# Leftover keys and values in half rows, AV over two PSUM banks, and batch 1's attention one block later, in a kernel of pooled attention and an MLP

## The chip, the cores and the metric

One core of one Trainium2 chip. The metric is the device time of the whole launch in microseconds (us), less is better. The kernel before takes 300.76 us (median of 3 runs, 300.65 to 300.78). All runs quoted here are of the fast state (some executions are slower at a lower granted clock, whatever the kernel; none of those is used); the profile's span is some 1.7 us shorter than the time.

## The reference

Eight batches of eight heads with 576 rows of 64. Keys and values are averaged over groups of 8 rows, so each head has 72 pooled keys. The attention output, 4608 tokens of 512, goes through an MLP with `h - tanh(h)` between its two products.

```python
k_p = k.reshape(B, H, Sp, pool, D).mean(axis=3)      # Sp = 72, pool = 8
v_p = v.reshape(B, H, Sp, pool, D).mean(axis=3)
attn = softmax(scale * q @ k_p.T)                    # (cut) max subtracted, 1e-9 added to the sum
x = (attn @ v_p).transpose(0, 2, 1, 3).reshape(B * S, H * D)
h = x @ w_in                                         # 512 -> 2048
return (h - np.tanh(h)) @ w_out                      # 2048 -> 512
```

## The kernel before

AV is the product of the attention weights and the pooled values; to "turn" a block is to transpose it on TensorE. PSUM, where TensorE writes, has eight banks. The MLP works on nine groups of 512 tokens. One group is a hidden phase (16 blocks of four matmuls of 512 columns) and an output phase (16 output blocks of four). The attention of batch 0 comes first, with nothing to hide it: this is the prelude. Batch 1's attention is hidden in group 0's output phase, the later ones in later groups. Two heads of pooled keys are 144 rows; 128 fill the partitions and 16 are "left". A batch has 4 pairs of heads, so 64 left rows. The queries of a head are 512 rows and a "tail" of 64.

```python
def load_dense(src, dst, b, eng=nc.sync):            # left rows of batch 0: 64 partitions, 2 KB each
    return eng.dma_start(out=dst[0 : NM * LO, NM, :], in_=src[b, 128:PR, :, :])

def load_q_tail(b, t, eng):                          # 64 rows x 8 heads: 512 pieces of 256 B
    eng.dma_start(out=t[:QT, :, R, :], in_=q[b, :, QA:S, :].rearrange("h p d -> p h d"))

def av_half(b, blk, half, x_sb, alloc):              # (cut) three matmuls into one PSUM bank, then
    nc.vector.reciprocal(out=rden[:, :, :], in_=ps[:, :, D:D1])
    nc.vector.tensor_tensor(out=x_sb[:, half, :, :], in0=ps[:, :, 0:D],
                            in1=rden[:, :, :].to_broadcast([128, 4, D]), op=ALU.mult)
# ... prelude (cut): ScalarE's program order
scores_wide(0, (0, 1))
nc.scalar.dma_start(out=t0[:QT, :, R, :], ...)       # batch 0's query tail, on ScalarE's queue
q_turn(nc.scalar.copy, 4, 6)
# ...
load_w2(0)                                           # GpSimd's queue: w1 in 4 chunks, then w2
load_w2(1)
after(load_k(1), w1_dmas[1])                         # SyncE: batch 1's keys once w1's 2nd chunk is in
load_q(1, False)
load_main(v_pairs, v_raw[1], 1, 0, NM)
# ... hidden phase of group 0
nc.scalar.copy(out=q_bf[:QT, R, :, :], in_=t0[:QT, :, R, :])   # cast of the tail, before block 0
for i in range(5, NHID):
    mlp_h(0, i, gts)
    if i == 7:  q_pe_tail(0)                         # its transposes
    if i == 9:  scores_tail(0)
    if i == 11: x4 = av(0, 4, ps_any, False)
    if i == 13: x_pe_transpose(0, 4, x4)
for u in range(16):                                  # output phase of group 0, batch 1 inside
    mlp_o(0, u % 4, (u // 4) * 4, (u // 4) * 4 + 4, gts, o_pools[u % 4])
    if u == 2: k_transpose(1, ...)
    # (cut)
    if u >= 11: x_pe_transpose(1, *pend.pop(0))
    # (cut)
```

Of the kernel before, what the change touches and what calls it, by code (L numbers as in the profile page):

```python
# [15 lines left out]
POOL = 8  # L16
# [3 lines left out]
R = 4  # L20
QA = 128 * R
QT = S - QA
T = B * S
# [14 lines left out]
def kernel(  # L38
# [19 lines left out]
    ps_h = ctx.enter_context(tc.tile_pool(name="ps_h", bufs=3, space=PSUM))  # L58
    ps_o = ctx.enter_context(tc.tile_pool(name="ps_o", bufs=2, space=PSUM))
    ps_a = ctx.enter_context(tc.tile_pool(name="ps_a", bufs=3, space=PSUM))  # L60
# [9 lines left out]

    w1b = const.tile([128, NFB, DFF], BF16, name="w1b")
# [3 lines left out]
    spread = const.tile([128, 128], BF16, name="spread")  # L75
    mask = const.tile([128, 3 * NM, 1], FP32, name="mask")
# [3 lines left out]
    q_bf = const.tile([128, R + 1, H, D], BF16, name="q_bf")  # L80
    warm = const.tile([128, 1], FP32, name="warm")
# [22 lines left out]
    def load_left(src, dst, b, eng=nc.sync):  # L104
        return [
            eng.dma_start(out=dst[32 * t : 32 * t + LO, NM, :], in_=src[b, 128:PR, t, :])
            for t in range(NM)
        ]
# [5 lines left out]

    def load_k(b):
        return [
            load_main(k_pairs, k_raw[b % 2], b, 0, NM),
            load_dense(k_pairs, k_raw[b % 2], b),
        ]

    def load_v(b):
        return [load_main(v_pairs, v_raw[b % 2], b, 0, NM)] + load_left(
            v_pairs, v_raw[b % 2], b
        )

    def load_q_tail(b, t, eng):
        eng.dma_start(
            out=t[:QT, :, R, :], in_=q[b, :, QA:S, :].rearrange("h p d -> p h d")
        )

    def load_q(b, tail=True):
        if b not in q_raws:
            q_raws[b] = raw.tile([128, H, R + 1, D], FP32, name="q_raw", tag="q_raw")
        t = q_raws[b]
        nc.sync.dma_start(
            out=t[:, :, 0:R, :], in_=q[b, :, 0:QA, :].rearrange("h (p j) d -> p h j d", j=R)
        )
        if tail:
            load_q_tail(b, t, nc.sync)
# [4 lines left out]
    def q_cast(b, eng=nc.gpsimd.tensor_copy, parts=1):  # L144
        t = q_raws.pop(b)
        n = H // parts
        for h in range(0, H, n):
            eng(  # L148
                out=q_bf[:, 0:R, h : h + n, :].rearrange("p j h d -> p h j d"),
                in_=t[:, h : h + n, 0:R, :],  # L150
            )
        eng(out=q_bf[:QT, R, :, :], in_=t[:QT, :, R, :])

    def q_dma_transpose(b):
        qT = work.tile([128, NHP, S], BF16, name="qT", tag="qT")
        for j in range(R + 1):
            rows = 128 if j < R else QT
            nc.sync.dma_start_transpose(
                out=qT[:, :, j * 128 : j * 128 + rows],
                in_=q_bf[:rows, j, :, :].rearrange("p h d -> p (h d)"),  # L160
            )
        qTs[b] = qT

    def q_pe_transpose(b, hps, eng=None):
        if b not in qTs:
            qTs[b] = work.tile([128, NHP, S], BF16, name="qT", tag="qT")
        qT = qTs[b]
        for hp in hps:
            ps = ps_any([128, QA], FP32, "qT_ps")
            for j in range(R):  # L170
                nc.tensor.matmul(  # L171
                    ps[:, j * 128 : (j + 1) * 128],
                    lhsT=q_bf[:, j, 2 * hp : 2 * hp + 2, :].rearrange("p h d -> p (h d)"),
                    rhs=ident[:, :],
                    start=True,
                    stop=True,
                )
            evac(qT[:, hp, 0:QA], ps[:, :], eng)

    def q_pe_tail(b):  # L180
        ps = ps_any([128, NHP, QT], FP32, "qt_ps")
        for hp in range(NHP):
            nc.tensor.matmul(
                ps[:, hp, :],
                lhsT=q_bf[:, R, 2 * hp : 2 * hp + 2, :].rearrange("p h d -> p (h d)"),
                rhs=ident[:, 0:QT],
                start=True,
                stop=True,
            )
        evac(qTs[b][:, :, QA:S], ps[:, :, :])  # L190

# [22 lines left out]
    def pool_v(b, eng):  # L214
# [10 lines left out]
        v_main(VB[b % 2], r[:, :, 0:1, :], eng, 0, NM)  # L225
        v_left(VB[b % 2], r[:, NM, 0:1, :], eng)

    def v_main(vb, vs, eng, t0, t1):
# [3 lines left out]
            in0=vs[:, t0:t1, :, :].to_broadcast([128, n, 2, D]),  # L232
# [4 lines left out]
        )  # L237

# [27 lines left out]

    def k_transpose(b, alloc, engs=(nc.vector.tensor_copy, nc.scalar.copy)):
# [5 lines left out]
        ps = alloc([128, 128], FP32, "kT_ps")  # L273
        turn_tile(ps[:, :], kd, NM)
# [18 lines left out]
    def score_mms(b, t, dst, c0, c1, pairs=range(NM)):  # L293
        for m in pairs if t == NM else (t,):
# [11 lines left out]
    def scores(b, t):  # L306
        if t == 0:
            E_tiles[b] = work.tile([128, NT, S], BF16, name="E", tag="E")
        E = E_tiles[b]
        hs = S // 2  # L310
        pss = []
        for half in range(2):
            ps = ps_a.tile([128, hs], FP32, name="s_ps", tag="ps_a")
            score_mms(b, t, ps[:, :], half * hs, (half + 1) * hs)
            pss.append(ps)
        for half, ps in enumerate(pss):
            nc.scalar.activation(  # L317
                out=E[:, t, half * hs : (half + 1) * hs], in_=ps[:, :], func=ACT.Exp, scale=SCALE
            )

    def scores_wide(b, ts):
# [3 lines left out]
        for t in ts:  # L325
            ps = ps_any([128, QA], FP32, "s_ps")
            score_mms(b, t, ps[:, :], 0, QA)
# [10 lines left out]
    def av_half(b, blk, half, x_sb, alloc):  # L338
        E = E_tiles[b]
        vb = VB[b % 2]  # L340
        c0 = blk * 128 if blk < 4 else S - 128
        ps = alloc([128, 4, D1], FP32, "x_ps")
        for n in range(3):
# [14 lines left out]
        rden = work.tile([128, 4, 1], FP32, name="rden", tag="rden", bufs=4)  # L358
        nc.vector.reciprocal(out=rden[:, :, :], in_=ps[:, :, D:D1])  # L359
        nc.vector.tensor_tensor(  # L360
            out=x_sb[:, half, :, :],
            in0=ps[:, :, 0:D],
            in1=rden[:, :, :].to_broadcast([128, 4, D]),
            op=ALU.mult,
        )
# [33 lines left out]
    def out_segments(c0, nrows):  # L399
        segs = []  # L400
        r = 0
        while r < nrows:
            c = c0 + r
            bb = c // S
            i = c % S
            if i < QA:
                j = i // 128
                p0 = i % 128
                ln = min(128 - p0, nrows - r, QA - i)
                dst = out[bb * S : bb * S + QA, :].rearrange("(p j) m -> p j m", j=R)[  # L410
                    p0 : p0 + ln, j, :
                ]
            else:
                ln = min(S - i, nrows - r)
                dst = out[bb * S + i : bb * S + i + ln, :]
# [6 lines left out]
    def mlp_h_mms(g, i, f0, f1, pool=None):  # L422
        tok0 = g * TG
        if f0 == 0:
            p, tag = pool or (ps_h, "hT_ps")
            h_tiles[i] = p.tile([128, TG], FP32, name="hT_ps", tag=tag)
# [96 lines left out]
    warm_ps = ps_o.tile([128, 512], FP32, name="warm_ps", tag="o_ps")  # L523
# [7 lines left out]
    t0 = raw.tile([128, H, R + 1, D], FP32, name="q_raw", tag="q_raw")  # L531

    def load_q0(h0, h1):
        return nc.scalar.dma_start(
            out=t0[:, h0:h1, 0:R, :],
            in_=q[0, h0:h1, 0:QA, :].rearrange("h (p j) d -> p h j d", j=R),
        )

    nc.vector.memset(zeros, 0.0)  # L539
    nc.vector.memset(k_raw[0][:, NM, :], 0.0)  # L540
    nc.vector.memset(v_raw[1][:, NM, :], 0.0)
    load_main(k_pairs, k_raw[0], 0, 0, 1)
    load_q0(0, 2)
    load_main(k_pairs, k_raw[0], 0, 1, 2)
    load_q0(2, 4)
    load_main(k_pairs, k_raw[0], 0, 2, 4)
    load_q0(4, 8)
    load_dense(k_pairs, k_raw[0], 0, nc.scalar)
    load_dense(v_pairs, v_raw[1], 0, nc.scalar)
# [7 lines left out]
    nc.gpsimd.memset(q_bf[64:128, R, :, :], 0.0)  # L557
# [16 lines left out]
    for i in range(2):  # L574
        nc.gpsimd.tensor_scalar_mul(VB[i][:, :, D:D1], mask[:, :, :], float(POOL))
    nc.gpsimd.dma_start(out=v_bf[:, 0:NM, :], in_=v_pairs[0, 0:128, :, :])  # L576
    nc.gpsimd.memset(spread[:, :], 0.0)
    nc.gpsimd.tensor_copy(
        out=spread.rearrange("p (t x) -> p t x", x=32)[:, :, 0:LO],
        in_=ident[:, 0 : NM * LO].rearrange("p (x t) -> p t x", t=NM),  # L580
# [4 lines left out]
    nc.gpsimd.tensor_copy(out=v_bf[:, NM, :], in_=v_raw[1][:, NM, :])  # L585
    load_w2(1)
    nc.gpsimd.memset(k_raw[1][:, NM, :], 0.0)
    nc.gpsimd.memset(v_raw[0][:, NM, :], 0.0)
    nc.gpsimd.memset(KB[1][:, :], 0.0)

    q_raws[1] = raw.tile([128, H, R + 1, D], FP32, name="q_raw", tag="q_raw")
    after(load_k(1), w1_dmas[1])
    load_q(1, False)
    load_main(v_pairs, v_raw[1], 1, 0, NM)

# [6 lines left out]
    def k_turn_left():  # L602
        ps = ps_any([128, 128], FP32, "kT_ps")
        turn_tile(ps[:, :], kdups[0], NM)
# [4 lines left out]
    def q_turn(eng, h0, h1):  # L609
        eng(  # L610
            out=q_bf[:, 0:R, h0:h1, :].rearrange("p j h d -> p h j d"),
            in_=t0[:, h0:h1, 0:R, :],
        )

    def v_pe_pool(t0, t1, turn):
        ps = ps_any([128, t1 - t0, 1, D], FP32, "v_ps")
        for j in range(POOL):
# [187 lines left out]
```

## Time and profile before

| kernel before | us |
|---|---|
| time, median of 3 runs | 300.76 |
| batch 0's first AV matmul | 14.61 |
| first hidden matmul of group 1, by the chain | 55.02 |
| the same, by its start in TensorE's timeline | 54.98 |
| span of the profile | 299.1 |

The prediction below shows the lines that carry the bound. Three lines that it did not look at matter afterwards. First two of ScalarE's timeline, then one of TensorE's (start, length, engine, line, operation, out<-in, shapes; in brackets the idle time before it and what ended it; ACTq and SPq are issues of transfers):

```profile
8.12 0.65 ACTq L640 DMA_DIRECT2D q_raw<-in_q_dram  x1
21.03 0.62 ACT L691 CAST q_bf<-q_raw 64x512 bf16<-64x512 f32 x1
```

```profile
26.02 0.28 PE L183 MATMUL qt_ps<-ident,q_bf 128*128 128x64 bf16 x4
```

There is no bracket on the last two. Batch 0's query tail, issued at 8.12 us on ScalarE's queue, lands 8.1 us later, and is long there when ScalarE casts it at 21.03 and when TensorE turns it at 26.02.

### The profile page before, as it was taken

What the parts mean: (1) busy time and instruction counts of PE and PEld (TensorE: products, weight loads), DVE (VectorE), ACT (ScalarE), POOL (GpSimd) and SP (SyncE); (2) the same over time, 40 slices, a digit from 0 to 9 for tenths busy, and PEclk for the clock granted to TensorE, in tenths of its full rate; (3) what the DMA queues carried; (4) which work ended last, traced back from release to release, by engine and by line L of the source; (5) the groups of instructions that cost most, each with busy time, mean ns of one, the idle gap of its engine ahead of it and who ended that gap; (6) DMA issues with size and microseconds to landing.
All of it is one profiled execution on the core that took longest, in us unless ns stands there. A gap on an engine that the chain in (4) does not pass through costs nothing.

```text
span 299.1 us, 4694 instructions
## 1 busy us (share of the span) xinstructions
PE 291.5 (97%) x1671; PEld 142.5 (48%) x1671; DVE 159.1 (53%) x343; ACT 149.4 (50%) x283; POOL 115.5 (39%) x110
## 2 busy tenths in 40 slices
PE   7989999999999999999999999999999999999994
PEld 3454455544544454445444554455445544444443
DVE  5658665673547444753476247716680758108600
ACT  4647583666146633654265516650665166126511
POOL 8500904871496109922971089307940000000000
PEclk9999999999999999999999999999999999999999
DMA  7999999849854998699648974897431430111032
GB/s 251 226 211 278 311 227 310 263 87 328 234 113 99 271 297 134 117 302 245 107 88 235 300 167 94 242 294 159 97 66 35 95 92 0 37 70 36 0 72 70
DMA packets 66183, 49.79 MB, mean 166 GB/s; under 512 B 39920, under 2 KB 52976, under 8 KB 66160
## 3 DMA queue, kind: packets, MB, share of 16 engines
q1 hardware_dynamic: 58832, 42.94, 56.0%
q0 software_dynamic: 4752, 4.72, 9.4%
q10 hardware_dynamic: 2576, 1.84, 2.3%
q8 instruction: 13, 0.21, 0.3%
q14 instruction: 10, 0.08, 0.1%
HBM read 36.70 MB, written 9.44 MB: 154 GB/s over the span
## 4 chain that ended last, share of the span: by engine, by line
PE 85%; DMA 9%; POOL 4%; issue 0%; SPq 0%; ACT 0%; DVE 0%; POOLq 0%
PE o_ps L456 40%; PE hT_ps L428 37%; DMA w1b<-in_moe_w_in_dram 4%; PE x_ps L346 4%; DMA k_raw<-in_k_dram 4%; PE s_ps L298 3%; POOL k_raw L198 1%; DMA out_dram<-o_sb 1%; POOL k_raw L203 1%; POOL kd L206 1%; POOL w2b L510 0%; PE xT_ps L390 0%; POOL v_raw L576 0%; PE qT_ps L171 0%; POOL w1b L503 0%
## 5 line engine op out<-in xcount | busy, mean ns | idle before, releaser
L456 PE MATMUL o_ps<-w2b,gT 128*128 128x512 bf16 x560 | 134.4, 380 | 0.0
L441 DVE TENSOR_TENSOR gT<-hT_ps,t_sb 128x512 bf16<-128x512 f32 x144 | 98.9, 691 | 57.7 <-ACT t_sb L439 57.6
L428 PE MATMUL hT_ps<-xT,w1b 128*128 128x512 bf16 x576 | 126.9, 379 | 0.3 <-ACT xT L397 0.3
L439 ACT ACTIVATE t_sb<-hT_ps 128x512 f32<-128x512 f32 x144 | 85.6, 597 | 38.3 <-PE hT_ps L428 37.5
L428 PEld LDWEIGHTS <-w1b 128*128 128x128 bf16 x576 | 55.9, 98 | 66.5 <-issue 0.4
L456 PEld LDWEIGHTS <-gT 128*128 128x128 bf16 x560 | 52.5, 98 | 52.0 <-issue 1.4
L465 ACT COPY o_sb<-o_ps 128x512 f32<-128x512 f32 x33 | 19.3, 585 | 75.2 <-PE o_ps L456 75.2
L359 DVE RECIPROCAL rden<-x_ps 128x4 f32<-128x4 f32 x80 | 14.2, 177 | 52.5 <-PE x_ps L346 52.0
L360 DVE TENSOR_TENSOR x_sb<-x_ps,rden 128x256 bf16<-128x256 f32 x80 | 34.0, 425 | 3.5 <-DMA xT<-x_sb 0.6
L148 POOL CAST q_bf<-q_raw 128x2048 bf16<-128x2048 f32 x6 | 11.3, 1888 | 59.9 <-issue 34.8
L198 POOL TENSOR_TENSOR k_raw<-k_raw 128x1280 f32<-128x1280 f32 x7 | 20.2, 2886 | 27.4 <-DMA k_raw<-in_k_dram 16.6
L317 ACT ACTIVATE E<-s_ps 128x288 bf16<-128x288 f32 x60 | 21.4, 410 | 13.2 <-PE s_ps L298 13.0
L346 PE MATMUL x_ps<-VB,E 128*128 128x130 bf16 x240 | 20.8, 221 | 0.4 <-ACT xT L397 0.3
L346 PEld LDWEIGHTS <-E 128*128 128x128 bf16 x240 | 16.9, 98 | 8.8 <-DVE VB L230 0.6
L216 POOL TENSOR_TENSOR v_raw<-v_raw 128x1280 f32<-128x1280 f32 x6 | 17.4, 2898 | 0.0
L298 PE MATMUL s_ps<-qT,KB 128*128 128x288 bf16 (+5 forms) x128 | 17.0, 290 | 0.2
L298 PEld LDWEIGHTS <-KB 128*128 128x128 bf16 (+1 forms) x128 | 7.0, 96 | 10.2 <-issue 3.5
L527 PE MATMUL warm_ps<-xT 128*128 128x512 bf16 x29 | 10.2, 465 | 1.3 <-DVE xT L539 1.3
L206 POOL TENSOR_TENSOR kd<-k_raw 128x640 bf16<-128x640 f32 x7 | 10.8, 1540 | 0.5
L203 POOL TENSOR_TENSOR k_raw<-k_raw 128x640 f32<-128x640 f32 x7 | 10.8, 1541 | 0.5
L397 ACT CAST xT<-xT_ps 128x256 bf16<-128x256 f32 (+1 forms) x14 | 5.8, 436 | 8.5 <-PE xT_ps L390 5.1
L219 POOL TENSOR_TENSOR v_raw<-v_raw 128x640 f32<-128x640 f32 x6 | 9.3, 1544 | 0.5
(73 smaller groups left out, 100.7 us busy)
## 6 DMA issues: line engine op xcount, KB each, us to landing
k_raw<-in_k_dram SPq DMA_DIRECT2D x7, 1024.0 KB, 5.9
q_raw<-in_q_dram SPq DMA_DIRECT2D x7, 1024.0 KB, 10.2
v_raw<-in_v_dram SPq DMA_DIRECT2D x7, 1024.0 KB, 9.3
out_dram<-o_sb SPq DMA_DIRECT2D x38, 128.0 KB, 2.4
out_dram<-o_sb SPq DMA_DIRECT2D x16, 256.0 KB, 3.7
w1b<-in_moe_w_in_dram POOLq DMA_DIRECT2D x4, 512.0 KB, 14.2
w2b<-in_moe_w_out_dram POOLq DMA_DIRECT2D x4, 512.0 KB, 16.9
k_raw<-in_k_dram SPq DMA_DIRECT2D x7, 128.0 KB, 5.8
```

The source lines that it names most:

```text
L198: first = eng.tensor_tensor(out=r[:, :, 0:4, :], in0=r[:, :, 0:4, :], in1=r[:, :, 4:8, :], op=ALU.add)
L216: eng.tensor_tensor(out=r[:, :, 0:4, :], in0=r[:, :, 0:4, :], in1=r[:, :, 4:8, :], op=ALU.add)
L298: nc.tensor.matmul(dst[p : p + w], lhsT=KB[b % 2][:, o : o + w], rhs=qTs[b][:, m, c0:c1], start=True, stop=True,)
L317: nc.scalar.activation(out=E[:, t, half * hs : (half + 1) * hs], in_=ps[:, :], func=ACT.Exp, scale=SCALE)
L346: nc.tensor.matmul(ps[:, 2 * n : 2 * n + 2, :].rearrange("p h d -> p (h d)") if n < 2 else ps.rearrange("p (a s) d -> p a s d", s=2)[:, :, ...
L359: nc.vector.reciprocal(out=rden[:, :, :], in_=ps[:, :, D:D1])
L360: nc.vector.tensor_tensor(out=x_sb[:, half, :, :], in0=ps[:, :, 0:D], in1=rden[:, :, :].to_broadcast([128, 4, D]), op=ALU.mult,)
L428: nc.tensor.matmul(h_tiles[i][:, :], lhsT=w1b[:, fb, i * 128 : (i + 1) * 128], rhs=xT[:, fb, tok0 : tok0 + TG], start=(fb == 0), stop=(fb ...
L439: nc.scalar.activation(out=t_sb[:, :], in_=h_ps[:, :], func=ACT.Tanh)
L441: nc.vector.tensor_sub(out=gT[:, :], in0=h_ps[:, :], in1=t_sb[:, :])
L456: nc.tensor.matmul(o_ps[:, :], lhsT=gts[i][:, tb * 128 : (tb + 1) * 128], rhs=w2b[:, i, :], start=(i == 0), stop=(i == NHID - 1),)
L465: (nc.vector.tensor_copy if g == 0 and tb % 2 else nc.scalar.copy)(out=o_sb[:, :], in_=o_ps[:, :])
```

## The change

The intent: use all 128 partitions for the left keys and values of the first two batches (each row of eight old rows cut into two halves of four, added by one fp32 matmul against a matrix `twos`), normalise two PSUM banks of AV with one instruction, and give batch 1's keys one more output block to arrive. Some transfers change their place in the queues to go with it. The diff, cut to its core:

```diff
+def load_halves(src, dst, b, eng=nc.sync):            # 128 partitions, 1 KB each
+    return eng.dma_start(out=dst[:, NM, 0:HALF], in_=src[b, 2 * 128 : 2 * PR, :, :])
+def turn_left(dst, b):                                # fp32: transposes and adds the halves
+    nc.tensor.matmul(dst, lhsT=k_left[b]..., rhs=twos[:, :], start=True, stop=True)
+def v1_left():                                        # batch 1's left values, fp32
+    nc.tensor.matmul(ps[:, 0, :], lhsT=spread32[:, :], rhs=vl[:, :], start=True, stop=True)
+def av_pair(p, half, b0):                             # two banks, one reciprocal, one multiply
+    nc.vector.tensor_tensor(out=x0[:, 2 * p : 2 * p + 2, half, :, :], in0=ps[:, :, :, 0:D], ...)
 # loads at the start
-load_dense(k_pairs, k_raw[0], 0, nc.scalar)
-load_dense(v_pairs, v_raw[1], 0, nc.scalar)
+load_halves(k_halves, k_raw[0], 0, nc.scalar)
+load_halves(v_halves, v_raw[1], 0, nc.scalar)
-nc.gpsimd.memset(q_bf[64:128, R, :, :], 0.0)          # was ahead of the value load on GpSimd
 nc.gpsimd.dma_start(out=v_bf[:, 0:NM, :], in_=v_pairs[0, 0:128, :, :])
+nc.gpsimd.memset(q_bf[64:128, R, :, :], 0.0)
-nc.scalar.dma_start(out=t0[:QT, :, R, :], ...)        # batch 0's query tail leaves ScalarE's queue
-load_w2(1)
-after(load_k(1), w1_dmas[1])
-load_q(1, False)
+k1 = load_main(k_pairs, k_raw[1], 1, 0, NM)
+after([k1], w1_dmas[1])
+load_halves(k_halves, k_raw[1], 1)
+load_halves(v_halves, v_raw[1], 1)
+load_q_tail(0)                                        # and comes behind batch 1's keys on SyncE's
+load_q_nine(1, 0, nc.sync)
+load_q_nine(1, 1, nc.sync)
 load_main(v_pairs, v_raw[1], 1, 0, NM)
+load_w2(1)
+after(w2_dmas[1:], k1)                                # w2's second chunk waits for batch 1's keys
 # hidden phase of group 0
-    if i == 7:  q_pe_tail(0)
-    if i == 9:  scores_tail(0)
-    if i == 11: x4 = av(0, 4, ps_any, False)
-    if i == 13: x_pe_transpose(0, 4, x4)
+    if i == 11: q_cast_tail(0, nc.scalar.copy)
+    if i == 12: q_four_tail(0)
+    if i == 14: scores_tail(0)
 # output phase: block 4 of batch 0 at u = 0 and 1; batch 1's steps one block later (its query tail four), so
-        if u >= 11: x_pe_transpose(1, *pend.pop(0))
+        if u >= 12: x_pe_transpose(1, *pend.pop(0))   # x block 3 after the 16th output block
+    # and block 4 inside group 1's hidden phase (i == 1)
```

All eight PSUM banks also become one tile that is cut by hand, and batch 1's queries are laid out in nine blocks of 64 rows. The key and value loads of some later batches are cut in two, so the change does touch something after group 1 begins; the result shows that this cost nothing.

> **What bounds the kernel now.** I read the page's engine shares first, then the chain that ended last, then TensorE's timeline of the first 55 us, then the DMA issues.
>
> ```profile
> PE 291.5 (97%) x1671; PEld 142.5 (48%) x1671; DVE 159.1 (53%) x343; ACT 149.4 (50%) x283; POOL 115.5 (39%) x110
> PE 85%; DMA 9%; POOL 4%; issue 0%; SPq 0%; ACT 0%; DVE 0%; POOLq 0%
> 30.21 2.90 POOL k_raw L198
> 37.82 0.45 PE kT_ps L259 x5
> 54.91 0.12 PE xT_ps L390 x4
> 55.02 13.93 PE hT_ps L428 x64
> ```
>
> The first two lines say that TensorE is the bound; the other four are pieces of the chain in order of time. After 37.8 us the chain is TensorE alone to the last output, and from 55.02 us each 64 matmuls of 512 columns take 13.81 us, so 216 ns each. Nothing after 55 us is touched by the change (the instruction orders of both kernels agree there, apart from four small transposes). So the whole question is **when the hidden-layer matmuls of token group 1 begin**, 55.02 us now; the 244 us behind it move along with it.
>
> TensorE's timeline, columns start, length, what, idle before it:
>
> ```profile
> 14.61 0.69 PE L346 MATMUL x_ps<-VB,E 128*128 128x130 bf16 x9
> 17.37 0.34 PE L346 MATMUL x_ps<-VB,E 128*128 128x130 bf16 x3 [0.29 <-ACT xT L397]
> 18.49 0.59 PE L428 MATMUL hT_ps<-xT,w1b 128*128 128x512 bf16 x2 [0.28 <-ACT xT L397]
> 20.41 5.78 PE L428 MATMUL hT_ps<-xT,w1b 128*128 128x512 bf16 x26
> 32.75 0.23 PE L390 MATMUL xT_ps<-ident,x_sb 128*128 128x64 bf16 x2 [0.32 <-DVE x_sb L360]
> 37.82 0.45 PE L259 MATMUL kT_ps<-ident,kd 128*128 128x128 bf16 x5 [0.52 <-POOL kd L206]
> ```
>
> Batch 0's first AV starts at 14.61, the prelude is over at 20.41, and then two holes are left: 0.32 us (last x of batch 0 waits for VectorE) and 0.52 us (batch 1's keys come late from GpSimd). The waits before 20.41, and the 20 filler matmuls ("warm_ps", 29 in all with the nine at the start) that stand in them, are where time can be won.
>
> ```profile
> 15.00 0.18 DVE L359 RECIPROCAL rden<-x_ps 128x4 f32<-128x4 f32 x1
> 15.22 0.42 DVE L360 TENSOR_TENSOR x_sb<-x_ps,rden 128x256 bf16<-128x256 f32 x1
> 19.63 0.43 DVE L360 TENSOR_TENSOR x_sb<-x_ps,rden 128x256 bf16<-128x256 f32 x1
> w2b<-in_moe_w_out_dram POOLq DMA_DIRECT2D x1, 512.0 KB, 24.4
> POOL k_raw L198 <- DMA k_raw<-in_k_dram: 16.6, 1, 16.6
> ```
>
> The eight normalisations of AV run on VectorE from 15.00 to 20.06. The second chunk of w2, issued at 11.31, lands 24.4 us later, at 35.7: the DMA row of the page reads 9 nearly throughout the first 50 us, so the queues are full as well. The last line is GpSimd's wait for batch 1's keys.
>
> **What the Trainium skill says.** "VectorE: DVE Perf Modes", section "The TRN2 errata", says that an instruction pays a fixed cost besides its elements; the trace agrees: 128x256 from PSUM takes 425 ns and 128x512 (the gT rows) 691, so 0.16 us are fixed. "FP8 and Floating Point Precision", section "TensorE Precision Notes", gives true fp32 four passes through the array; no run here shows it yet. "DMA: Bandwidth & Descriptors", section "Queues, rings and completion order", says that an engine takes turns between its queues. The packets agree: from 25 to 28 us, 279 packets of 2 KB from SyncE's queue and 278 of 1 KB from GpSimd's moved, one for one, so 10.8 ns a pair, while GpSimd's queue alone (41 to 42 us) moved 197, so 5 ns each.
>
> **The change, part by part.**
>
> 1. Left keys of batch 0. VectorE's three additions (0.43 + 0.58 + 0.29 us, 10.47 to 11.83) become two of 128x128 at 0.29 each, so they end near 11.1. One bf16 turn becomes an fp32 matmul of 64 columns: 4 x 64 columns at 0.42 ns is 0.11 us, [...] I estimate 0.3 us. The third and fourth query transposes no longer stand behind two fillers, which lets ScalarE begin copying at 10.15 and not 10.50. Walking through: third score near 11.7, left scores 11.95, their exp done at 13.05 (now 13.76). The left values need 4 matmuls, not 8, and the eight 256-column pooling matmuls (13.04 to 14.1) become two sets of eight at 128 columns, the first ready at 13.25. First AV at about **13.75 in place of 14.61**.
>
> 2. Two-bank AV. Eight reciprocal-and-multiply pairs, 0.555 us apart in the trace, become four of 0.18 + 0.69 less overlap, 0.83 apart. First one ready 15.15, last 17.65 (now 20.06). The transposes of half 0 (two ScalarE copies of 128x512, 0.59 each) finish at 17.05, and from there TensorE has work without a hole: ten half-done hidden matmuls (2.16 us) and eight transposes (0.45) bring it to **19.7 with 54 hidden matmuls left**. Now 54 are left at 20.41 + 4 x 0.216 = 21.27. Gain 1.6 us, of which TensorE keeps every bit only if nothing later is late.
>
> 3. Hidden phase to output phase. 19.7 + 54 x 0.216 + 0.24 + 0.35 (query tail, score tail) = 31.95. The w1 chunks come sooner than now, as no small transfers run beside them on ScalarE's queue. Batch 0's last AV block now stands in the output phase; VectorE reaches it after the last gT, which I put 0.5 us late (now 0.32): -0.2.
>
> 4. Batch 1's keys. They should land at about 27.9 (now 29.4 and 30.05, since they wait for the second w1 chunk, some 1 us earlier). GpSimd then issues w2's second chunk (0.75), pools 4/5 of the old elements (2.35 + 1.3 + 1.3), issues the third (0.75), pools the left halves (2 x 0.45): main keys at 33.7, left ones at 35.5. They are asked for one block later, at 31.95 + four blocks (3.45) + AV (0.35) + transposes and hole (0.8) = 36.5. So the 0.52 us hole goes: +0.5. The fp32 turn and the fp32 left-value matmul cost about 0.25 us each: -0.5.
>
> 5. w2's second chunk. It now waits for batch 1's keys. In the trace a GpSimd transfer issued at 33.05 to 33.8 moved its first packet at 37.1, so 3.3 us after the issue. Issued to 28.65 it would start at 32.0, take turns with batch 1's values (512 pairs at 10.3 ns, 5.3 us) and land near 37.6, estimate 36.8 to 37.8. It is asked for at about 37.1. That makes a new wait of 0 to 0.7: -0.35.
>
> 6. Batch 1 one block later. The last x block that group 1 needs (block 3) is now transposed right after the sixteenth output block, and the first hidden matmul of group 1 must wait for ScalarE's copy. Now block 3 is turned one block earlier (53.82), and 0.86 us of output matmuls cover the copy. From the trace: transposes to modelled end 0.39, copy 0.59, hand-over 0.08, of which 0.22 is work: **a new hole of 0.84 us** at the seam, which no other work covers. Block 4 moves behind it at equal cost.
>
> Sum: +1.6 - 0.2 + 0.5 - 0.5 - 0.35 - 0.85 = +0.2; about 0.2 of TensorE's small unexplained gaps before 39.5 us and an earlier w2 would add up to 0.5 more. I take a gain of 0.55 us: **300.2 us**.
>
> **Rivals.**
>
> A. *The prelude's gain arrives whole.* If w2's second chunk lands by 36.8 and the hole at the seam is short, group 1 begins some 1.6 us earlier: 299.1. For it: TensorE is 97% busy and the old holes have clear causes that the change addresses. Against it: the copy between transposes and hidden matmuls stands in the program order.
>
> B. *Weights become the bound.* GpSimd issues three of four w2 chunks after batch 1's keys, and everything is on saturated DMA. If each chunk is 1 us later than I worked out, the wait at the fifth output block eats 1.5 us and the sum turns negative: 301.3. For it: the trace's 8.7 us from issue to landing of w2's third chunk. Against: chunks three and four have over 1 us of slack in my timeline.
>
> C. *fp32 matmuls are dear.* If they cost 0.8 us and not 0.3, the prelude loses 0.5 and the output phase 1.0: 301.5. Nothing in the trace speaks to it, as no fp32 matmul runs now.
>
> D. *Steady state shifts.* All PSUM becomes one tile. If its dependencies were coarser, every group would pay. Against: the waits listed in both instruction orders are alike from group 1 on, and TensorE's idle time there is 0.0.
>
> **Range and chances.** The certain gain (1.6 + 0.5) and the certain new costs (0.2 + 0.5 + 0.85) nearly cancel; the w2 wait (0 to 0.7), the fp32 size (0.2 to 0.8 each) and the prelude's end (plus or minus 0.5) give about 1.1 us either way: 299.1 to 301.3. Two per cent is 6 us, more than all that the first 20 us could yield, so "within 2%" is nearly certain: 0.97, with 0.02 for faster and 0.01 for slower.
>
> **What would show it.** Right: first AV near 13.75; four multiplies of about 690 ns over 128x512; the continuous run of hidden matmuls from about 17 us; GpSimd's keys ready before they are asked for; a hole before the first hidden matmul of group 1 put down to ScalarE's xT copy; group 1 beginning near 54.5. Wrong: that hole absent or below 0.4 us; a wait for w2 over 1 us; an fp32 matmul over 0.6 us; idle time on TensorE after group 1 has begun; a run outside 299.1 to 301.3.

## The result, and the profile after

The changed kernel took 302.49 us (median of 4 runs, 302.21 to 302.51) against 300.70 (300.37 to 300.78) of the kernel before on the same chip: ratio 1.0059, 95% interval 1.0042 to 1.0077. Ratios here are the mean time of one kernel's fast runs over that of the other's of the same rounds, so not quite the ratio of the medians quoted. The prediction said 300.2 and at most 301.3: the time rose where a small gain was expected.

Group 1 begins at 56.84 us in place of 54.98 (starts in TensorE's timeline), 1.86 later, and that is all of the loss. TensorE's timeline of the changed kernel:

```profile
14.24 1.21 PE L507 MATMUL PS<-VB,E 128*128 128x130 bf16 x18
19.50 10.34 PE L580 MATMUL PS<-xT,w1b 128*128 128x512 bf16 x45
31.46 0.29 PE L230 MATMUL PS<-ident,q_bf 128*128 128x64 bf16 x4 [1.62 <-ACT q_bf L207]
37.21 0.23 PE L543 MATMUL PS<-ident,x_sb 128*128 128x64 bf16 x2 [0.32 <-DVE x_sb L493]
39.23 0.39 PE L412 MATMUL PS<-twos,k_left 128*128 128x64 f32 x2
39.45 1.03 PE L608 MATMUL PS<-w2b,gT 128*128 128x512 bf16 x4
56.84 1.89 PE L580 MATMUL PS<-xT,w1b 128*128 128x512 bf16 x8 [0.67 <-ACT xT L550]
```

The third line is the surprise: a hole of 1.62 us ahead of the transposes of batch 0's query tail, released by ScalarE's cast. ScalarE's timeline names what the cast waited for:

```profile
9.60 1.14 ACT L201 CAST q_bf<-q_raw 128x512 bf16<-128x512 f32 x2 [0.86 <-DMA q_raw<-in_q_dram]
30.78 0.62 ACT L207 CAST q_bf<-q_raw 64x512 bf16<-64x512 f32 x1 [1.17 <-DMA q_raw<-in_q_dram]
```

The tail landed at 30.8. SyncE's own queue says why (start and length of each issue; a long one contains a wait):

```profile
0.81 16.94 SPq L142 DMA_DIRECT2D k_raw<-in_k_dram  x4
17.79 0.68 SPq L156 DMA_DIRECT2D k_raw<-in_k_dram  x1
18.57 0.85 SPq L156 DMA_DIRECT2D v_raw<-in_v_dram  x1
19.47 0.64 SPq L188 DMA_DIRECT2D q_raw<-in_q_dram  x1
```

The fourth key load is held until w1's second chunk is in, at 17 us, and the tail stands behind it and behind two half-row loads. It is issued at 19.47 where it was issued at 8.12 before, and takes 11.3 us to land where it took 8.1. The prelude, the first term of the prediction's sum, is in VectorE's timeline:

```profile
10.80 0.29 DVE L333 TENSOR_TENSOR k_raw<-k_raw 128x128 f32<-128x128 f32 x1 [0.53 <-DMA k_raw<-in_k_dram]
15.11 0.69 DVE L826 TENSOR_TENSOR x<-PS,rden 128x512 bf16<-128x512 f32 x1
17.63 0.69 DVE L826 TENSOR_TENSOR x<-PS,rden 128x512 bf16<-128x512 f32 x1
```

The four multiplies last 690 ns and follow each other 0.84 apart, as predicted. But the first one ends at 15.8 and not at 15.15, and the first AV began at 14.24 and not at 13.75: the last query cast and the left keys had waited for transfers (0.86 and 0.53 us, the brackets above). Run 3 shows how little of this lateness those waits explain.

### The profile page after: what moved, and what is told of

It is laid out like the page before. It is cut to its first block, busy times and chain, and to the rows that moved or that the text cites. A ratio compares the mean times of both kernels' runs of the same rounds, so it can differ in the third digit from the quotient of the medians.

```text
span 300.8 us, 4686 instructions
## 1 busy us (share of the span) xinstructions
PE 289.4 (96%) x1641; PEld 142.8 (47%) x1673; DVE 156.9 (52%) x333; ACT 148.6 (49%) x279; POOL 115.7 (38%) x116
## 4 chain that ended last, share of the span: by engine, by line
PE 84%; DMA 8%; DVE 2%; POOL 2%; issue 1%; ACT 1%; SPq 1%; POOLq 0%; DVEq 0%; ACTq 0%
PE PS L608 39%; PE PS L580 37%; PE PS L507 4%; DMA q_raw<-in_q_dram 4%; DMA w1b<-in_moe_w_in_dram 4%; PE PS L451 3%; DVE x_sb L493 1%; DMA out_dram<-o_sb 1%; SPq L156 1%; DVE rden L492 0%; POOL v_raw L720 0%; PE PS L264 0%; POOL w1b L655 0%; DVE gT L593 0%; DVE o_sb L617 0%
## 5 line engine op out<-in xcount | busy, mean ns | idle before, releaser
L608 PE MATMUL PS<-w2b,gT 128*128 128x512 bf16 x542 | 131.9, 379 | 0.9 <-issue 0.2
L593 DVE TENSOR_TENSOR gT<-PS,t_sb 128x512 bf16<-128x512 f32 x144 | 99.0, 691 | 60.4 <-ACT t_sb L591 60.2
L580 PE MATMUL PS<-xT,w1b 128*128 128x512 bf16 x564 | 126.1, 379 | 1.6 <-ACT xT L550 0.7
L591 ACT ACTIVATE t_sb<-PS 128x512 f32<-128x512 f32 x144 | 85.6, 597 | 38.8 <-PE PS L580 38.1
L617 ACT COPY o_sb<-PS 128x512 f32<-128x512 f32 x33 | 19.3, 585 | 76.6 <-PE PS L608 75.3
L201 POOL CAST q_bf<-q_raw 128x2048 bf16<-128x2048 f32 x6 | 11.3, 1888 | 59.0 <-issue 35.4
L493 DVE TENSOR_TENSOR x_sb<-PS,rden 128x256 bf16<-128x256 f32 x72 | 30.6, 425 | 2.5
L469 ACT ACTIVATE E<-PS 128x288 bf16<-128x288 f32 x60 | 21.4, 410 | 13.2 <-PE PS L451 13.0
L301 POOL TENSOR_TENSOR k_raw<-k_raw 128x1280 f32<-128x1280 f32 (+1 forms) x7 | 19.7, 2808 | 12.5 <-DMA k_raw<-in_k_dram 12.5
L507 PE MATMUL PS<-VB,E 128*128 128x130 bf16 x240 | 20.4, 220 | 0.5 <-ACT E L484 0.2
L451 PE MATMUL PS<-qT,KB 128*128 128x288 bf16 (+5 forms) x128 | 17.0, 289 | 0.3
```

What stands on the lines that cost most here:

```text
L301: first = eng.tensor_tensor(out=r[:, :, 0:4, :], in0=r[:, :, 0:4, :], in1=r[:, :, 4:8, :], op=ALU.add)
L451: nc.tensor.matmul(dst[p : p + w], lhsT=KB[b % 2][:, o : o + w], rhs=qTs[b][:, m, c0:c1], start=True, stop=True,)
L469: nc.scalar.activation(out=E[:, t, c0:c1], in_=ps, func=ACT.Exp, scale=SCALE)
L507: nc.tensor.matmul(ps[:, 2 * n : 2 * n + 2, :].rearrange("p h d -> p (h d)") if n < 2 else ps.rearrange("p (a s) d -> p a s d", s=2)[:, :, ...
L580: nc.tensor.matmul(h_tiles[i][:, :], lhsT=w1b[:, fb, i * 128 : (i + 1) * 128], rhs=xT[:, fb, tok0 : tok0 + TG], start=(fb == 0), stop=(fb ...
L591: nc.scalar.activation(out=t_sb[:, :], in_=h_ps[:, :], func=ACT.Tanh)
```

## The experiments

Twelve kernels ran, in four calls. The kernel before ran beside them each time (medians 300.75, 300.66, 300.70 and 300.92). All results were correct. Theory A: the cost is where batch 0's query tail stands in the queue, plus the seam hole that was predicted. The rivals are named in the expectations. The changed kernel did not run again in these calls, so a difference from its 302.49 is one between medians of different calls.

### 1. The tail early, from ScalarE's queue

```diff
     scores_wide(0, (0, 1))
+    load_q_tail(0, nc.scalar)
...
-    load_q_tail(0)
```

> Changed kernel with one thing undone: batch 0's query tail (512 pieces of 256 B) is loaded from ScalarE's queue right after the first two scores, as in the kernel before, and not from SyncE's queue behind batch 1's keys. Theory A (the tail's place in the queue made ScalarE wait until 30.8 us and TensorE stop before 31.46): the hole before the query-tail transposes goes, 302.5 becomes 300.7 (-1.8, the hole of 1.6 idle plus refill). Rival B (the queues are full, so the tail's 512 pieces only push something else later: they take turns with the w1 chunks, the keys of batch 1 come later and TensorE waits for those): the hole moves to w1, the keys or w2, and the time stays above 302.0.

Measured 305.74 us (305.21 to 306.41), ratio 1.016: a miss. My edit brought a wait of its own. ScalarE's timeline in this run:

```profile
11.94 0.65 ACTq L188 DMA_DIRECT2D q_raw<-in_q_dram  x1
12.63 1.14 ACT L201 CAST q_bf<-q_raw 128x512 bf16<-128x512 f32 x2 [3.75 <-DMA v_raw<-in_v_dram]
```

ScalarE could not issue the tail before the left values had landed, and stood 3.75 us. The wait is not for the tail's own data. In the trace's operands, the tail's issue waits for and later signals on one semaphore (109), the one on which the left values' load signals its end; that load landed at 11.92, and the issue began at 11.94. The hole at the tail's transposes did fall to 0.33 us, but the prelude was 4.04 later. TensorE stood 3.55 us in it, and then had half its clock, as the windows show (columns: stretch, its length, busy time of PE, PEld, DVE, ACT, POOL, granted clock, DMA share, GB/s):

```profile
10.00:13.00 3.00, 0.00 (x0) 0.00 (x0) 0.95 (x4) 0.37 (x1) 1.02 (x4) 1.00 1.23 210
13.00:16.00 3.00, 2.70 (x14) 1.83 (x14) 0.00 (x0) 2.29 (x5) 1.40 (x4) 0.52 1.24 206
```

So this run settles nothing on the time; it says where the tail must not be issued.

### 2. The seam

x block 3 of batch 1 is turned before the sixteenth output block, into a free bank, so that four output matmuls cover ScalarE's copy.

```diff
+        if u == 15:
+            x_pe_transpose(1, *pend.pop(0), ps=bank(3, [128, 4, 128]))
         mlp_o(0, tb, qd * 4, qd * 4 + 4, gts, o_pools[tb])
```

> Changed kernel, but the four transposes of batch 1's x block 3 stand ahead of the sixteenth output block of group 0 (into a PSUM bank that is free there), not behind it. Theory A (the hole before group 1 is ScalarE's copy laid bare): the 0.84 us between the transposes and the first hidden matmul of group 1 go, 302.5 becomes 301.7. Rival B (VectorE's normalising of block 3 is what is late, so that the transposes only wait earlier): a hole of like size before the transposes, time unchanged.

Measured 301.63 us (301.37 to 301.82), ratio 1.0021, so 0.86 below the changed kernel by the medians. TensorE's timeline has no bracket at the first hidden matmul of group 1 any more:

```profile
56.17 1.89 PE L581 MATMUL PS<-xT,w1b 128*128 128x512 bf16 x8
```

From the start of the tail's transposes to the start of group 1 this profile takes 24.56 us (31.61 to 56.17) and the changed kernel's 25.38 (31.46 to 56.84): 0.82 less. The prediction's 0.85 for this term is right.

### 3. The value load later

GpSimd clears a buffer before it issues batch 0's value load, as in the kernel before.

```diff
+    nc.gpsimd.memset(q_bf[64:128, R, :, :], 0.0)
     nc.gpsimd.memset(mask[:, :, :], 1.0)
     ...
     nc.gpsimd.dma_start(out=v_bf[:, 0:NM, :], in_=v_pairs[0, 0:128, :, :])
-    nc.gpsimd.memset(q_bf[64:128, R, :, :], 0.0)
```

> Changed kernel with GpSimd's memset of the query tail's rows back ahead of batch 0's value load, as before, so that this load is issued about 0.5 us later. Theory A (half of why the prelude gained 0.9 us and not 1.6: the value load reaches the queues 0.7 us sooner and takes turns with the last queries and the left keys): ScalarE's third query cast starts near 9.0 and not 9.6, first AV about 0.4 us earlier, and 0.4 us off the time, unless the query tail's hole swallows it (that hole hangs on the first two w1 chunks, not on the prelude), in which case the time stays at 302.5 and only the profile shows it. Rival B (the half rows alone delay it, twice the pieces at one turn each): third cast still at 9.6.

Measured 302.36 us (302.23 to 302.63), ratio 1.0048. The last query cast started at 8.96 and not 9.60, the left keys waited for no transfer, the first AV came at 14.06 and the long run of hidden matmuls began at 19.33, 0.17 earlier. TensorE then only waited longer for the tail:

```profile
31.60 0.29 PE L230 MATMUL PS<-ident,q_bf 128*128 128x64 bf16 x4 [1.93 <-ACT q_bf L207]
```

So two things are shown: the earlier value load did delay the queries and left keys that the prelude waits for, though with those waits mostly gone the first AV still comes 0.31 after the predicted 13.75; and while the tail is late no gain of the prelude reaches the end.

### 4. AV normalised bank by bank

```diff
-        nc.vector.reciprocal(out=rden[:, :, :, :], in_=ps[:, :, :, D:D1])
-        nc.vector.tensor_tensor(out=x0[:, 2 * p : 2 * p + 2, half, :, :], ...)
+        for k in range(2):
+            nc.vector.reciprocal(out=rden[:, k, :, :], in_=ps[:, k, :, D:D1])
+            nc.vector.tensor_tensor(out=x0[:, 2 * p + k, half, :, :], ...)
```

> Changed kernel with batch 0's AV normalised a bank at a time (eight reciprocals and eight multiplies, as before) and all else kept. Theory A (two-bank AV is worth 4 x (2 x 0.555 - 0.83) = 1.1 us on VectorE, and the query tail's hole takes the gain back since the tail lands at the same time): the last multiply ends about 1.1 us later, the hole before the query tail shrinks by as much, and the time stays within 0.3 of 302.5. Rival B (the gain of the prelude reaches the end): 303.5.

Measured 302.79 us (302.17 to 303.24), ratio 1.0058, 0.3 above the changed kernel by the medians and equal by the ratios. The time hardly moves, as in run 3. The profile is no clean comparison, as one part of a key load was late in it (see run 5). So the worth of the merged multiply had to be asked again in run 9.

### 5. The tail early, from SyncE's queue

The tail's load comes ahead of batch 1's keys on SyncE's queue, once batch 0's values have landed.

```diff
+    after([load_q_tail(0)], v0)
     k1 = load_main(k_pairs, k_raw[1], 1, 0, NM)
...
-    load_q_tail(0)
```

> The changed kernel with batch 0's query tail ahead of batch 1's keys in SyncE's queue, issued when batch 0's values have landed (about 12.3 us), so that no engine but SyncE waits to issue it (the trial that issued it from ScalarE made ScalarE wait 3.75 us). Theory A (its place behind the keys made the hole): it lands near 20, of the 2.0 us that TensorE lost before the query-tail transposes 0.3 are left (ScalarE's cast itself), and the time falls by up to 1.7; but then the fifth output block is asked for at 37.8 and w2's second chunk lands at 38.2 to 38.8 (keys issued a little later), so 0.4 to 1.0 of it comes back as a wait there: 301.2 to 301.9. Rival B (full queues: everything only moves): w1 or the keys come later and the time stays at 302.5.

Measured 301.57 us (300.91 to 302.01), ratio 1.0028, 0.9 below the changed kernel. The hole is nearly gone:

```profile
31.00 0.29 PE L230 MATMUL PS<-ident,q_bf 128*128 128x64 bf16 x4 [0.33 <-ACT q_bf L207]
```

The time fell by less than the hole. It lies in the range that I expected, but not for my reason: the wait for w2 that I had counted in does not show. In the profiled run the prelude was late (the long run of hidden matmuls began at 20.33, not at 19.50): 15 of the 16 parts of batch 0's third key load had ended by 7.17, the last one at 8.60. In run 7 all had ended by 7.23. Some profiles show this and others do not, in kernels with the same start; what decides it stays open. The profiles of runs 2, 4, 5, 6 and 12 show it. It moves the prelude by some 0.8 us, which the tail's hole hides where there is one, and I take it (without a test) for the spread of the runs that have none.

### 6 and 7. All mends together, without and with w2's second chunk early

Run 6 joins runs 2, 3 and 5 and casts the tail one block earlier. Run 7 also issues w2's second chunk right behind the first, as the kernel before does.

```diff
     load_w2(0)
+    load_w2(1)
...
-    load_w2(1)
-    after(w2_dmas[1:], k1)
```

> The same, with block 3's transposes ahead of the sixteenth output block, the value load issued 0.5 us later, and ScalarE's cast of the query tail one hidden block earlier so that it is done when TensorE asks. Theory A: another -0.85 from the seam and -0.3 from the cast, but w2's second chunk now lands over 1 us after it is asked for and takes the cast's gain: 300.2 to 301.0, a wait of 1 to 1.6 us before the fifth output block.

> The same again, with w2's second chunk issued directly behind the first, as in the kernel before. Theory A: the wait before the fifth output block goes; group 1 begins at about 53.6 and the time is 299.3 to 299.9, better than the kernel before (300.7). Rival B (w2's second chunk takes turns with batch 1's keys and queries, which then come late): a wait at batch 1's key or query transposes of the same size, time as in the run without this.

Run 6 took 300.44 us (300.11 to 300.83), ratio 0.9994. The wait for w2 that I expected there (1 to 1.6 us) is not in its profile, but only by luck: the prelude of that profile was late by 0.86, and w2's second chunk, issued at 28.28, landed 9.9 us later, at 38.2, just as the fifth output block began, at 38.25. With a prelude in time, that block would have waited some 0.8 us (an estimate from these numbers). In run 7 the chunk landed at 36.7 and the block began at 37.38. Run 7 took **299.76 us** (299.49 to 300.34), ratio 0.9972, 95% interval 0.996 to 0.9983: it beats the kernel before by 0.9 us. ScalarE's cast of the tail, and then TensorE's timeline:

```profile
28.36 0.60 ACT L207 CAST q_bf<-q_raw 64x512 bf16<-64x512 f32 x1
```

```profile
19.22 10.34 PE L581 MATMUL PS<-xT,w1b 128*128 128x512 bf16 x45
29.39 0.28 PE L230 MATMUL PS<-ident,q_bf 128*128 128x64 bf16 x4
53.93 1.89 PE L581 MATMUL PS<-xT,w1b 128*128 128x512 bf16 x8
```

No bracket stands on these. Group 1 begins 1.05 us earlier than before. The two runs differ by 0.7 us, but part of that can be the late part of the key load, so I do not put a measured number on w2's place.

### 8. Batch 1 back to the block where it was

Run 7 with batch 1's attention one output block earlier, as in the kernel before, and so without the special place for x block 3.

```diff
-        if u == 3:
+        if u == 2:
             k_transpose(1, ps_any, (nc.vector.tensor_copy, nc.vector.tensor_copy))
```

(and likewise for every later step)

> As the last one, but instead of moving block 3's transposes, batch 1's whole attention stands one output block earlier, as in the kernel before. If the shift was needed for the data: waits for batch 1's keys (ready about 35) or queries (cast done about 37) at the third and fourth output blocks, 0.5 us or more, 299.9 to 300.5. If it was not needed: like the last one, 299.3 to 299.9, and the seam needs no other cure.

Measured 300.04 us (299.93 to 300.47), ratio 0.9982, 0.3 above run 7, though the runs of the two overlap; in the profiles group 1 begins 0.48 later (54.41 and 53.93). TensorE waits once, for ScalarE, and ScalarE had waited for batch 1's queries:

```profile
35.52 1.05 ACT L240 CAST q_b<-q_raw 128x1024 bf16<-128x1024 f32 x1 [2.28 <-DMA q_raw<-in_q_dram]
38.04 0.61 PE L264 MATMUL PS<-ident,q_b 128*128 128x128 bf16 x8 [0.52 <-ACT xT L550]
```

The releaser of the second line is ScalarE's copy of batch 0's last x block, which stands behind the casts of the queries. So the extra block takes away a wait of about half a microsecond. It is not the wait that the prediction meant: batch 1's keys are turned at 36.05 here, a block earlier, without a wait. Where it brought the seam hole with it, it cost more than it gave.

### 9. Bank by bank again, without the tail's hole

Run 7 with the edit of run 4.

> The fastest version so far (299.76) with AV normalised bank by bank, eight pairs of instructions on VectorE and not four. With the tail's hole gone nothing swallows a later prelude. Theory A (the merged multiply is worth 0.25): 300.0, at most 300.3. Rival (the prediction's: it carries most of 1.6 us): 300.9 or more.

Measured 300.16 us (299.68 to 301.15), ratio 0.9986 against 0.9972 of run 7, so 0.4 us. In the profile the long run of hidden matmuls began 0.26 later than in run 7:

```profile
19.48 10.34 PE L581 MATMUL PS<-xT,w1b 128*128 128x512 bf16 x45
```

The merged multiply is worth 0.26 us in the profile and 0.4 in time (the runs of the two overlap), not most of 1.6.

### 10. The tail put back

Run 7 with the tail's load and cast where the changed kernel has them.

> The fastest version so far (299.76) with batch 0's query tail put back where the changed kernel has it: behind batch 1's keys, cast at the later block. Everything else stays. Theory A: the hole before the tail's transposes returns, 1.9 to 2.5 us, less the 0.33 that is there anyway; 301.5 to 302.0. Rival: other waits had already covered it and it costs under 0.8: 300.5 or less.

Measured 305.03 us (303.71 to 306.96), ratio 1.0149: 5.3 us above run 7, over twice what I expected. TensorE's timeline and its windows:

```profile
33.12 0.29 PE L230 MATMUL PS<-ident,q_bf 128*128 128x64 bf16 x4 [3.60 <-ACT q_bf L207]
36.03 1.89 PE L581 MATMUL PS<-xT,w1b 128*128 128x512 bf16 x4
```

```profile
33.60:35.50 1.90, 1.90 (x8) 0.69 (x6) 1.24 (x2) 0.82 (x2) 0.76 (x2) 0.72 1.05 389
35.50:38.00 2.50, 2.50 (x15) 1.10 (x14) 0.83 (x2) 0.97 (x3) 0.00 (x0) 0.53 1.14 290
```

The tail's cast here starts at 32.45, 1.7 later than in the changed kernel; w2's earlier second chunk on GpSimd's queue is the other difference ahead of it that I see, though no run tells that apart. The hole grew to 3.60 us, so the tail's transposes come 3.73 later than in run 7, and after that TensorE's clock was halved for some 3.4 us, from about 34.4 (the shares 0.72 and 0.53 come out so): four hidden matmuls took from 36.03 to the first output matmul at 37.71, 420 ns each and not 216. The output phase begins 5.25 us later than in run 7, which is the difference in time. The Trainium skill says this in "TensorE: Matmul & The Clock Gate", section "What's actually happening": the array's clock is halved after an idle window of about 3.4 us. This case agrees: after 1.62 us (the changed kernel) the granted clock is 1.00, after 3.55 and 3.60 it is 0.52 and 0.53. It is why this direction of the test exaggerates the tail's cost: the one of the six runs with a mean clock of 0.999 took 303.71, the others (0.989 to 0.994) 304.78 to 306.96.

### 11 and 12. The kernel before with the tail alone moved

The tail's load goes behind batch 1's keys, and its cast, transposes, scores and AV block 4 go to the blocks of the changed kernel. Nothing else of the change is in it. In run 11 batch 1's tail stays on ScalarE's queue; in run 12 it moves as well, behind batch 1's queries.

```diff
-nc.scalar.dma_start(out=t0[:QT, :, R, :], ...)
 after(load_k(1), w1_dmas[1])
+load_q_tail(0, t0, nc.sync)
-load_q(1, False)
+load_q(1)                                 # run 12 only, with its line on ScalarE's queue taken out
...
+    if i == 11: nc.scalar.copy(out=q_bf[:QT, R, :, :], in_=t0[:QT, :, R, :])
+    if i == 12: q_pe_tail(0)
+    if i == 14: scores_tail(0)
```

> The kernel before with one part of the change alone: batch 0's query tail is taken from ScalarE's queue and put on SyncE's behind batch 1's keys, and its cast, transposes, scores and the last AV block stand at the hidden blocks of the changed kernel. Theory A (the position of that transfer is what costs): in the kernel before the keys land at 29.4 and 30.05, so the tail's pieces end near 31 to 32; TensorE asks for the transposes near 31.1 (46 matmuls after 21.3), so a wait of 0.5 to 1.7 appears there, put down to ScalarE's cast; time 301.1 to 302.4. Rival (the loss belongs to the half rows and the fp32 matmuls, and the tail only shows it): no wait over 0.4 and a time within 0.3 of the kernel before.

> The run before_tail again without the wait that my edit brought there (ScalarE could not issue batch 1's query tail until batch 1's keys had landed, 27.6 us; TensorE stood 11 us): that tail is now loaded on SyncE's queue behind batch 1's queries. The kernel before with batch 0's query tail behind batch 1's keys, its consumers at the changed kernel's blocks. Theory A: TensorE asks for the tail's transposes near 30.3 (42 matmuls after 21.3) and the tail lands near 31 to 31.5, so a hole of 0.8 to 2.2 put down to ScalarE's cast; 301.0 to 302.6. Rival (the loss belongs to the half rows and the fp32 matmuls): hole under 0.4, within 0.4 of the kernel before.

Run 11 took 319.46 us (317.55 to 320.25), ratio 1.0613, and failed like run 1. ScalarE's timeline:

```profile
27.60 0.65 ACTq L127 DMA_DIRECT2D q_raw<-in_q_dram  x1
28.28 0.92 ACT L397 CAST xT<-xT_ps 128x256 bf16<-128x256 f32 x3 [14.06 <-DMA k_raw<-in_k_dram]
```

ScalarE could not issue batch 1's tail until batch 1's keys had landed, and the rest of the prelude stood behind that issue. Here too the trace's operands show one shared semaphore (100): the keys landed at 27.57, the issue began at 27.60. The run says nothing of theory A.

Run 12 took 303.18 us (301.85 to 304.14), ratio 1.0071, 95% interval 1.0044 to 1.0097: 2.3 us above the kernel before on the same chip. ScalarE's timeline and TensorE's:

```profile
32.55 0.62 ACT L698 CAST q_bf<-q_raw 64x512 bf16<-64x512 f32 x1 [1.78 <-DMA q_raw<-in_q_dram]
```

```profile
33.23 0.29 PE L183 MATMUL qt_ps<-ident,q_bf 128*128 128x64 bf16 x4 [2.23 <-ACT q_bf L698]
```

The hole of the changed kernel is there without half rows, without fp32 matmuls and without two-bank AV. This shows theory A: moving that transfer and its users, in the kernel before, opens the hole. Group 1 begins 2.09 us later than in the kernel before (57.07 and 54.98), of which 0.25 is a late prelude (20.66 and 20.41), so the tail costs 1.8 us there. The 2.3 in time, 0.6 over my upper bound, holds a second cost: three of the six runs have a mean clock of 0.994 and took 303.51 to 304.14, the three at 0.998 or more took 301.85 to 302.85. A mean lower by 0.006 over 301 us is what one halving of 3.4 us takes away, as in run 10; these runs were not profiled, so that it was the hole that brought it on is not shown.

## Why the prediction was wrong

**The view was right.** Only the start of group 1 mattered: it moved by 1.86 us and the medians by 1.79. Rival D (a coarser steady state) did not happen: from group 1's start to the end of the span the two kernels take the same time (244.1 and 244.0 us), though later loads are cut in two, which "Nothing after 55 us is touched" had missed.

**The step that failed is part 3.** It added up "19.7 + 54 x 0.216 + 0.24 + 0.35 (query tail, score tail) = 31.95", which counts the tail's work but never asks when its data come. The sentence after it, "The w1 chunks come sooner than now, as no small transfers run beside them on ScalarE's queue", saw that the small transfers had moved, and took only the gain of it. The tail had been put behind a load that waits until 17 us for w1, and landed at 30.8. In run 7 the same stretch, from the long run's start to the tail's transposes, takes 10.17 us (19.22 to 29.39); in the changed kernel 11.96 (19.50 to 31.46). So the term left out is **1.8 us**, and runs 5 and 12 show it from both sides: without this place in the queue the hole goes, and with it alone the hole comes.

**Part 1 and 2, the prelude, had the right mechanism and the wrong size.** With 54 hidden matmuls left, the kernel before stood at 21.27 and the changed one at 20.36 (19.50 and four matmuls): 0.9 gained, where 1.6 was predicted. Part 1 counted 0.86 up to the first AV, and it was 0.37: the first AV came at 14.24 and not 13.75. Run 3 won 0.18 of that back by issuing the value load later; the rest stays open (that the half rows' pieces cost something was not tested). Part 2 counted 0.7 from there on, and it was 0.53 (6.66 us before, 6.13 after), of which the two-bank multiply alone is worth 0.26 to 0.4 (run 9).

**Part 4 was right.** The keys were there when asked for: 0.5 us won. In run 8 they are there without the extra block as well, so it was not the shift that won it (the main keys landed at 27.2 where it was 29.4 before). The fp32 matmuls at 39.23 and 46.83 take 0.22 and 0.27 us from their start to the next one's: 0.5 in all, as predicted. Rival C is out.

**Part 5, the wait for w2's second chunk, did not come** (0.35 predicted): the fifth output block begins at 39.45 without a bracket. That is luck. The chunk, issued at 27.46, landed 10.6 us later, at 38.1, past the estimate of 36.8 to 37.8. (Part 5 also uses 10.3 ns a pair where its own packets give 10.8.) The block was asked for late, because of the tail's 1.8 us; without them it would have been asked for near 37.65 and have waited some 0.4 (an estimate). So the term was right and the tail's hole hid it. Rival B is out for the changed kernel.

**Part 6, the seam, was right** (0.84 predicted; 0.86 by the medians and 0.82 in the profile of run 2).

The new sum: +0.9 - 1.8 + 0.5 - 0.5 - 0.85 = -1.75, against 1.79 measured in time and 1.86 at the start of group 1. A hole of 0.32 us before the last x of batch 0 is unchanged, so the 0.2 set down for it fell away; the move of AV block 4's transposes behind group 1's start gives back 0.1, and somewhat more goes in gaps, one of them 0.25 us before 51.67, where an AV matmul waits for ScalarE's exponentials.

## What to carry to other kernels

When a change moves a small transfer to another queue, work out when it lands and compare that with when its first user asks for it, even where the profile of before shows no wait for it: a missing bracket says only that it was early enough at its old place. Changes that make an early stage faster give nothing while a later wait is for data that come at a fixed time; take that wait away first, then measure the others. And in an experiment that moves a DMA issue onto a computing engine's queue, look first whether the engine itself must wait before it can issue; in both cases here it waited for another transfer's semaphore, which the new issue was to use too. And a wait that does not show may only be hidden by another one: compare when the data landed with when they were asked for.

## What the Trainium skill lacked or had wrong

- "TensorE: Matmul & The Clock Gate", section "What's actually happening", says that the window runs free and that the point of transition varies by up to 500 ns either way. It does not say how long after a hole the halving can still come. In run 10 TensorE worked again from 33.12, and the clock fell at about 34.4, for some 3.4 us.
- "FP8 and Floating Point Precision", section "TensorE Precision Notes", counts four passes for fp32 but gives no time for a small matmul. Here one of 128x64 leaves two matmul records, and the next instruction starts 0.22 to 0.31 us after it.
- "DMA: Bandwidth & Descriptors", section "Queues, rings and completion order", describes the turns between queues but not what they mean for a small transfer behind big ones: 128 KB in 512 pieces of 256 B, issued at 19.47 us behind three loads on a busy queue, landed at 30.8.
- "DMA: Bandwidth & Descriptors", section "Latency and other measured facts", does say that two of the 16 DMA engines are usually slower. It lacks a size: here the last of the 16 parts of one load came 1.43 us after the others in one profile (run 5) and not late in another (run 7). Whether one of those two engines moved it is not known.
- No page puts a size on what a computing engine loses when an issue on its queue must wait for the semaphore of an earlier transfer: 3.75 us in run 1 and 14.06 us in run 11.
